# Each DMA transposition of u (128 x 1024) issued as two of 512 columns, in a fused retention and SoLU kernel on one core

## The chip, the cores and the metric

The kernel runs on 1 core of one Trainium2 chip. The metric is the device time of one execution in microseconds (us), measured outside the profiler; less is better. Before the change it is 212.93 us, the median of 3 runs (211.94 to 213.08). Where a profile is quoted, it is one execution taken by the hardware profiler, and its span runs from the first to the last instruction.

## The reference

A retention step (attention without softmax, with a decaying causal mask) feeds a feed-forward layer with the SoLU activation and a normalisation:

```python
# q, k, v: (8, 8, 576, 64) float32
scores = (1 / sqrt(64)) * (q @ k.T)
gamma  = 1 - 2 ** (-5 - head)
ret    = scores * where(i >= j, gamma ** (i - j), 0)
x      = (ret @ v) as (4608, 512)          # 8 batches x 576 tokens, 8 heads x 64

h  = x @ w_in                              # (4608, 1024)
e  = exp(h - max(h));  sm = e / sum(e)
s  = h * sm
ln = (s - mean(s)) / sqrt(var(s) + 1e-6) * g_ln
out = ln @ w_out                           # (4608, 512) float32
```

The inputs are drawn at random, x 0.1 for q, k and v.

## The kernel before, in words

The 4608 tokens are cut into 36 chunks of 128 tokens: for each pair of batches eight full chunks and one that holds the last 64 tokens of both. A chunk passes through some thirty small steps, each a Python function of the chunk's number:

- `ld` (L265 to L275) loads q, k and v of a chunk, 256 KB each, by three DMAs on SyncE's queue (L270 and L274).
- `cq`, `ck`, `cv` convert them to 16 bits with the decay factored in, on GpSimd, VectorE or ScalarE.
- `tq`, `tr` and `eq`, `er` transpose q and k on TensorE and copy the result out. For some later chunks `kd` (L322) transposes k by a DMA instead, 128 x 512 to 128 x 4 x 128 (L326), and `kq` (L330) does the same for q of one chunk (L331).
- `sc`, `mk`, `av`, `fs`, `ex` compute scores, mask, ret @ v and the carried state; `m1` computes h = x @ w_in on TensorE; `mx`, `xp`, `so` compute max, exp and u = -h * e (`so`, VectorE, L527).
- u (128 tokens x 1024, 16 bits, 256 KB) has to be transposed before the last product. For 19 of the 36 chunks `tu` (TensorE) and `eu` (a copy out of PSUM) do this, and for the last chunk steps of its own in halves. For the other 16, `du` (L592) does it by one DMA on SyncE's queue (L594).
- `m2` multiplies uT by w_out in 8 blocks of 128 rows, two matmuls a block through the helper `product` (L256). `st` scales the result by 1/sqrt(var) on ScalarE (L615) and stores it on SyncE's queue (L621, L623).

The order of all steps on all engines is a list written out by hand (ORDER, L24): a token such as `du:23` issues that step for chunk 23, and every engine works through its own instructions in the order of this list. SyncE issues all loads, all stores and all DMA transpositions, in that order too: an instruction of SyncE that waits holds all those behind it. Buffers are named by hand as well (RINGS and SLOTS): u and uT have 5 buffers each, the loads 6 or 7, the output 4. Each DMA signals its landing on one of eight semaphores, taken in turn, and waits before its issue for the DMA that used the same semaphore eight DMAs earlier.

The 16 uses of `du` begin at 95.4 us. They are thin at first (chunks 12, 14, 16, 18) and dense in the second half of the list.

Of the kernel before, what the change touches and what calls it, by code (L numbers as in the profile page):

```python
# [146 lines left out]
def kernel(  # L147
# [10 lines left out]
    nc = tc.nc  # L158
# [71 lines left out]
    def ring(pool, shape, dtype, name):  # L230

        at = int(next(slots[name]))
        assert at < RINGS[name]
        return pool.tile(shape, dtype, tag=f"{name}_{at}", name=name, bufs=1)
# [5 lines left out]
    T = {}  # L240
# [350 lines left out]

    def du(n):  # L592
        uT = ring(utp, [P, NF, P], F16, "uT")
        nc.sync.dma_start_transpose(out=uT, in_=T.pop(("u", n)))  # L594
        T["uT", n] = uT

    def eu(n, e="a"):
# [268 lines left out]
```

## Time and profile before

| what | value |
|---|---|
| time, median of 3 runs | 212.93 us (211.94 to 213.08) |
| profiled execution, its span | 210.9 us |
| TensorE (PE) busy | 194.3 us, 92% |
| VectorE (DVE) busy | 181.4 us, 86% |
| ScalarE (ACT) busy | 170.5 us, 81% |
| GpSimd (POOL) busy | 157.2 us, 75% |
| granted TensorE clock | 1.000 |
| SyncE's DMA queue, packets' time | 99.7% of 16 engines' span |
| DMA transpositions of u (L594) | 16, issued from 95.4 to 198.2 us |
| DMA transpositions of k (L326) and q (L331) | 7 and 1 |

The profiled execution's own time outside the span is not recorded; the span lies 2.0 us under the median of the runs.

How to read the profile: PE is TensorE's matmuls, PEld its weight loads, SPq is SyncE's queue, which issues DMAs. A line number is that of the source before the change. In the groups, `out<-in xcount | busy, mean ns | idle before` gives the work of one line and the time in which its engine stood idle in front of it. In the timeline of SyncE a row has its start, its length and the DMA that it issues; the length covers the issue and whatever held it up. In the chain of waits each row has its start, its length and the work to which that time is put down. A wait reads as who waited, for whom, the total in us, how often, and the longest.

### The profile page before, as it was taken

The numbers are of one execution on the slowest core, as the hardware profiler recorded it, in microseconds if no ns is written. First come the engines' busy times: TensorE is split into PE (matmuls) and PEld (weight loads), VectorE is DVE, ScalarE is ACT, GpSimd is POOL, SyncE is SP. The second block draws the span as 40 slices with busy tenths as digits, with TensorE's granted clock in tenths as the row PEclk, the third lists the DMA queues.
The fourth block names the chain that finished last, engine by engine and source line by source line (L and its number), as shares of the span: only waits on it lengthen the run. The fifth ranks groups of instructions, "written<-read, shape, count | busy, mean of one in ns | idle before, by whom it ended". The sixth has DMA issues, their size and how long they took to land.

```text
span 210.9 us, 7583 instructions
## 1 busy us (share of the span) xinstructions
PE 194.3 (92%) x3125; PEld 124.0 (59%) x3125; DVE 181.4 (86%) x323; ACT 170.5 (81%) x299; POOL 157.2 (75%) x226
## 2 busy tenths in 40 slices
PE   0887798999999999999999999999999998999992
PEld 0464476575666657657566667575656654565562
DVE  0486999979997999899989999999879998999760
ACT  2424999898979999999898978999679976677981
POOL 5377899676689899888839798879999977545620
PEclk9999999999999999999999999999999999999999
DMA  5999998999898989999999899999989999899754
GB/s 134 257 330 294 258 272 290 253 209 299 224 215 258 265 215 273 221 251 230 208 275 197 205 231 238 273 226 206 179 143 256 210 166 205 156 247 199 154 174 149
DMA packets 110834, 47.71 MB, mean 226 GB/s; under 512 B 94536, under 2 KB 104784, under 8 KB 110800
## 3 DMA queue, kind: packets, MB, share of 16 engines
q1 hardware_dynamic: 110480, 47.07, 99.7%
q8 instruction: 24, 0.39, 0.8%
q10 hardware_dynamic: 320, 0.16, 0.3%
q14 instruction: 10, 0.08, 0.2%
HBM read 32.54 MB, written 9.44 MB: 199 GB/s over the span
## 4 chain that ended last, share of the span: by engine, by line
PE 55%; SPq 14%; DMA 8%; DVE 8%; POOL 7%; ACT 3%; issue 3%; DVEq 0%; POOLq 0%
PE o L256 21%; PE h L256 18%; SPq L274 5%; SPq L270 5%; DMA w_out<-in_moe_w_out_dram 3%; PE tp L251 3%; PE sc L381 3%; PE lp L251 3%; DMA qkT<-k 2%; PE x L456 2%; POOL v L279 2%; SPq L789 2%; DMA qf<-in_q_dram 2%; PE x L256 2%; SPq L779 2%
## 5 line engine op out<-in xcount | busy, mean ns | idle before, releaser
L256 PE MATMUL h<-w_in,xT 128*64 128x512 f16 x560 | 66.9, 380 | 0.1
L256 PE MATMUL o<-w_c,uT 128*64 128x512 f16 x480 | 56.9, 380 | 0.0
L394 DVE TENSOR_TENSOR ret<-sc,tris 128x512 f16<-128x512 f32 x72 | 46.1, 682 | 2.8 <-PE sc L381 2.5
L256 PEld LDWEIGHTS <-xT 128*64 128x64 f16 x576 | 31.5, 110 | 23.1 <-issue 0.7
L512 DVE TENSOR_REDUCE nm<-h 128x1 f32<-128x1024 f32 x35 | 42.6, 1216 | 2.8 <-PE h L256 2.7
L256 PEld LDWEIGHTS <-uT 128*64 128x64 f16 x560 | 31.0, 110 | 23.0 <-issue 0.6
L527 DVE SCALAR_TENSOR_TENSOR u<-h,e 128x1024 f16<-128x1024 f32 x35 | 42.5, 1215 | 1.5 <-ACT e L518 1.4
L518 ACT ACTIVATE e<-h,nm 128x1024 f32<-128x1024 f32 x35 | 39.4, 1125 | 5.0 <-DVE nm L512 3.1
L432 POOL TENSOR_TENSOR s<-t,small 128x512 f16<-128x512 f32 x32 | 33.9, 1063 | 7.4 <-DVE t L420 6.1
L555 ACT ACTIVATE sq<-u,su 128x1024 bf16<-128x1024 f16 x30 | 34.8, 1159 | 2.0 <-DVE u L527 2.0
L581 POOL TENSOR_TENSOR rs<-w,mhalf 128x1 f32<-128x1 f32 x36 | 20.3, 570 | 20.7 <-DVE w L572 17.2
L290 POOL TENSOR_TENSOR q<-qf,small 128x512 f16<-128x512 f32 x30 | 31.2, 1043 | 5.4 <-DMA qf<-in_q_dram 5.1
L279 POOL TENSOR_TENSOR v<-vf,small 128x512 f16<-128x512 f32 x30 | 31.7, 1062 | 2.8 <-DMA vf<-in_v_dram 2.5
L615 ACT ACTIVATE o_sb<-o,rs 128x512 f32<-128x512 f32 x35 | 24.0, 692 | 4.5 <-POOL rs L581 3.2
L243 ACT COPY qkT<-tp 128x512 f16<-128x512 f16 x42 | 23.0, 599 | 5.0 <-PE tp L251 4.9
L243 ACT CAST xT<-x 128x512 f16<-128x512 f32 x29 | 17.1, 593 | 3.1 <-PE x L256 2.8
L251 PE MATMUL tp<-ident,q 128*64 128x128 f16 x232 | 12.4, 230 | 6.0 <-POOL q L290 5.5
L243 ACT CAST k<-kf 128x512 f16<-128x512 f32 x17 | 10.5, 626 | 7.7 <-DMA kf<-in_k_dram 7.7
L456 PE MATMUL x<-ret,v 128*64 128x128 f16 x288 | 14.8, 222 | 2.1 <-DVE ret L394 1.5
L251 PEld LDWEIGHTS <-q 128*64 128x64 f16 x280 | 11.0, 115 | 8.9 <-POOL q L290 5.7
L381 PE MATMUL sc<-qkT 64*128 64x128 f16 x288 | 14.7, 223 | 1.3 <-DMA qkT<-k 0.8
L444 POOL TENSOR_TENSOR s<-t,small 128x256 f32<-128x256 f32 x24 | 15.3, 638 | 0.9 <-DVE t L420 0.8
(87 smaller groups left out, 272.1 us busy)
## 6 DMA issues: line engine op xcount, KB each, us to landing
qf<-in_q_dram SPq DMA_DIRECT2D x36, 256.0 KB, 5.1
kf<-in_k_dram SPq DMA_DIRECT2D x36, 256.0 KB, 5.0
vf<-in_v_dram SPq DMA_DIRECT2D x36, 256.0 KB, 5.5
out_dram<-o_sb SPq DMA_DIRECT2D x35, 256.0 KB, 4.2
w_in<-in_moe_w_in_dram SPq DMA_DIRECT2D x4, 512.0 KB, 6.0
w_out<-in_moe_w_out_dram SPq DMA_DIRECT2D x4, 512.0 KB, 6.5
uT<-u SPq DMA_TRANSPOSE x16, 4.6
out_dram<-o_sbh SPq DMA_DIRECT2D x2, 64.0 KB, 1.8
```

Source lines behind the costliest of these rows:

```text
L243: (engine.copy if engine is nc.scalar else engine.tensor_copy)(out=out, in_=in_)
L251: nc.tensor.transpose(out=out[w], in_=in_[:, w], identity=ident)
L256: nc.tensor.matmul(out=out[w], lhsT=lhsT[:, w], rhs=rhs, start=start, stop=stop, skip_group_check=True,)
L279: engine.tensor_tensor(out=dst, in0=T.pop((key, n)), in1=table.unsqueeze(2).to_broadcast([P, H, D]), op=ALU.mult,)
L290: ENG[e].tensor_tensor(out=dst.rearrange("p (a h) d -> p h a d", h=2), in0=T.pop(("qf", n)).rearrange("p (h a) d -> p h a d", h=2), in1=ta ...
L394: nc.vector.tensor_tensor(out=r, in0=s, in1=m, op=ALU.mult)
L432: nc.gpsimd.tensor_tensor(out=s16, in0=t.unsqueeze(2).to_broadcast([P, 4, 2, D]), in1=gd.unsqueeze(3).to_broadcast([P, 4, 2, D]), op=ALU.mult,
L512: nc.vector.tensor_reduce(out=nm, in_=T["h", n], axis=AX.X, op=ALU.max, negate=True)
L518: nc.scalar.activation(out=e, in_=T["h", n], func=ACT.Exp, bias=T.pop(("nm", n)), accum_out=s)
L527: nc.vector.scalar_tensor_tensor(out=u, in0=T.pop(("h", n)), scalar=-1.0, in1=T.pop(("e", n)), op0=ALU.mult, op1=ALU.mult, accum_out=su,)
L555: nc.scalar.activation(out=s, in_=T.pop(("v", n)), func=ACT.Square, scale=-float(DFF), bias=T.pop(("su", n)), accum_out=ss,)
L615: nc.scalar.activation(out=o_sb, in_=T.pop(("o", n)), func=ACT.Copy, scale=T.pop(("rs", n)))
```

## The change

`du` takes its tile of u, allocates the same buffer for uT, and issues two DMAs in place of one: columns 0 to 511 go into blocks 0 to 3 of uT, columns 512 to 1023 into blocks 4 to 7. Both stand on SyncE's queue, one directly behind the other. The tokens in ORDER, the buffers and all other steps are unchanged.

```diff
     def du(n):
         uT = ring(utp, [P, NF, P], F16, "uT")
-        nc.sync.dma_start_transpose(out=uT, in_=T.pop(("u", n)))
+        u = T.pop(("u", n))
+        for i in range(2):
+            nc.sync.dma_start_transpose(
+                out=uT[:, 4 * i : 4 * i + 4], in_=u[:, 512 * i : 512 * i + 512]
+            )
         T["uT", n] = uT
```

In the program that results, SyncE has 16 instructions more. The first half carries the waits of the old DMA (for u, and for the last product that read the buffer of uT). The second half waits only for the DMA eight places earlier in the queue. On TensorE the product `m2` waits for the first half before its first block and for the second half before its fifth. The order of the instructions on every engine is otherwise as it was; the DMAs behind each split take the next semaphores of the eight in turn.

## The prediction

> **What bounds the kernel now.** I read the page first, then the busy time by stage, then the chain of waits, and last the timeline of SyncE, the only queue that the edit touches. From the page:
>
> ```profile
> span 210.9 us, 7583 instructions
> ...
> PE 55%; SPq 14%; DMA 8%; DVE 8%; POOL 7%; ACT 3%; issue 3%; DVEq 0%; POOLq 0%
> ...
> L256 PE MATMUL o<-w_c,uT 128*64 128x512 f16 x480 | 56.9, 380 | 0.0
> ```
>
> TensorE carries most of the chain, SyncE's queue comes second. The third line is the consumer of the transposed u: 480 matmuls, and TensorE stood idle 0.0 us in front of them, so no uT arrives late today. By stage (us; then PE, PEld, DVE, ACT, POOL busy with counts; clock; DMA share and GB/s):
>
> ```profile
> 139.00:177.00 38.00, 37.24 (x617) 23.71 (x613) 35.41 (x61) 31.51 (x57) 32.85 (x48) 1.00 1.08 201
> 177.00:195.00 18.00, 17.18 (x224) 9.48 (x222) 16.69 (x29) 13.57 (x24) 10.12 (x14) 1.00 1.09 199
> 195.00:211.00 16.00, 12.08 (x158) 7.51 (x154) 7.76 (x23) 10.47 (x21) 4.74 (x12) 1.00 0.58 159
> ```
>
> From 139 to 195 us TensorE is idle for 0.76 + 0.82 us only, at full clock. Whatever stops TensorE there is paid at the end, nearly one for one. The DMA share of 1.08 says that packets were under way on all 16 engines together nearly all the time. What stops TensorE, from the waits:
>
> ```profile
> PE sc L381 <- DMA qkT<-k: 0.8, 1, 0.8
> ...
> POOL q L279 <- DMA qf<-in_q_dram: 2.6, 1, 2.6
> ```
>
> and from the chain (start, us, what):
>
> ```profile
> 173.57 5.15 DMA qkT<-k
> 178.71 0.05 issue
> 178.76 0.40 PE sc L381 x8
> ...
> 199.71 3.45 PE o L256 x32
> 203.16 0.45 PE lph L251 x16
> 203.61 1.73 PE o L256 x16
> 205.33 1.77 PE oh L256 x32
> ```
>
> So there is one place where SyncE already sets the end: the transposition of k issued at 173.57, landed at 178.71, on which the score matmuls wait. It stands behind everything that SyncE issued earlier, five transpositions of u in this stage among them. After 178.76 the chain is TensorE alone.
>
> **The price of one split.** The two kinds of transposition that the trace has, by source line (min/median/max ns):
>
> ```profile
> L594 SPq DMA_TRANSPOSE uT<-u x16: 1238/1440/3667, 95.4 to 198.2; - x16
> ...
> DMA to landing us min/median/max: 3.4/4.6/5.7
> ...
> L326 SPq DMA_TRANSPOSE qkT<-k x7: 1195/1224/2036, 143.0 to 176.9; - x7
> ```
>
> L326 moves 512 columns, the very shape of a half; L594 moves 1024. SyncE needs at least 1195 ns for the one and 1238 for the other: its time hardly depends on the columns. So a half is priced at 1.20 us, the first half replaces the old instruction, and the second adds 1.20 and about 0.08 to the next row (152.47 + 1.30 to 153.89 below is 0.12, 169.15 + 1.39 to 170.60 is 0.06): 1.28 us each, 16 x 1.28 = 20.5 us of SyncE. Bytes do not change. On the DMA engines I take two halves to cost what one whole costs: the program's own 512-column transpositions show nothing else.
>
> **How much of it is hidden.** SyncE works in order, and many of its rows last longer than their floor (1.24 for a whole transposition, 1.20 for 512 columns, 0.53 for a store, 0.57 for a load at L274). I call the excess a hold: the DMA queue is full and SyncE waits for room. That is an inference, from the DMA share above; the waits view names compute engines for some of these rows, without a pattern. A hold can hide the extra issue in front of it, since SyncE would stand there anyway. The decisive stage:
>
> ```profile
> 140.74 2.16 SPq L594 DMA_TRANSPOSE uT<-u  x1
> ...
> 146.94 3.53 SPq L594 DMA_TRANSPOSE uT<-u  x1
> ...
> 152.47 1.30 SPq L594 DMA_TRANSPOSE uT<-u  x1
> 153.89 2.04 SPq L326 DMA_TRANSPOSE qkT<-k  x1
> ...
> 158.17 1.14 SPq L621 DMA_DIRECT2D out_dram<-o_sb  x1
> 159.42 1.33 SPq L326 DMA_TRANSPOSE qkT<-k  x1
> ...
> 162.81 3.67 SPq L594 DMA_TRANSPOSE uT<-u  x1
> ...
> 169.15 1.39 SPq L594 DMA_TRANSPOSE uT<-u  x1
> 170.60 0.57 SPq L274 DMA_DIRECT2D qf<-in_q_dram  x1
> 171.22 1.30 SPq L274 DMA_DIRECT2D kf<-in_k_dram  x1
> 172.56 0.90 SPq L274 DMA_DIRECT2D vf<-in_v_dram  x1
> 173.57 1.72 SPq L326 DMA_TRANSPOSE qkT<-k  x1
> ```
>
> Five splits: 5 x 1.28 = 6.40 us. Holds on other rows: 0.84 (153.89), 0.61 (158.17), 0.13 (159.42), 0.73 (171.22), 0.33 (172.56), 0.52 (173.57), together 3.16. Holds on the split rows themselves: 0.92, 2.29 and 2.43 at 140.74, 146.94 and 162.81, almost nothing on the other two. Two bounds follow for the delay at 173.57:
>
> - All holds hide. Carried forward: 1.28 - 0.92 = 0.36, gone at 146.94; 1.28 - 0.06 = 1.22 after 152.47, 0.38 after 153.89, gone at 158.17; nothing left of 162.81; 1.13 after 169.15, 0.40 after 171.22, 0.07 after 172.56, gone at 173.57. The delay is 0.
> - Holds on split rows hide nothing, because the second half waits for the same room as the whole did and spends its 1.20 after that: 6.40 - 3.16 = 3.24.
>
> I take the middle. A half asks for half the room, so the first half can go in during the hold, but the second still ends after it: half of 1.28 hidden at each of three long holds, 1.92. The delay is 6.40 - 1.92 - 3.16 = 1.32, rounded to **1.3 us**, at the transposition on which TensorE waits with nothing to spare (landed 178.71, used 178.76). The load of 170.60 feeds GpSimd, which stood 2.6 us for it; it is late by about as much and ends on the same chain.
>
> **Before 139 us** the four splits are followed by larger holds:
>
> ```profile
> 99.78 2.89 SPq L621 DMA_DIRECT2D out_dram<-o_sb  x1
> 102.77 1.33 SPq L594 DMA_TRANSPOSE uT<-u  x1
> ...
> 109.70 3.26 SPq L621 DMA_DIRECT2D out_dram<-o_sb  x1
> ```
>
> A store of 0.53 that lasts 2.89 or 3.26 us has over 2.3 us of hold; one split in front of each needs 1.28. Price 0; if that cover is gone, 1.28 falls on the loads behind each, whose buffers are several chunks ahead.
>
> **After 177 us** six more splits and the last one:
>
> ```profile
> 180.84 1.05 SPq L270 DMA_DIRECT2D qf<-in_q_dram  x1
> ...
> 183.32 2.68 SPq L594 DMA_TRANSPOSE uT<-u  x1
> 186.10 1.00 SPq L621 DMA_DIRECT2D out_dram<-o_sb  x2
> 187.20 3.93 SPq L594 DMA_TRANSPOSE uT<-u  x2
> 191.22 0.53 SPq L621 DMA_DIRECT2D out_dram<-o_sb  x1
> 191.86 2.69 SPq L594 DMA_TRANSPOSE uT<-u  x2
> ...
> 198.19 1.24 SPq L594 DMA_TRANSPOSE uT<-u  x1
> ```
>
> From 179.5 to 194.55 there are 6 x 1.28 = 7.7 us more and holds of about 1.44 (183.32) + 1.45 (the pair at 187.20, 3.93 less two floors) + 0.4 (180.84) = 3.3, so the last of this group is issued 4.4 us later. It would end at about 199; the quickest landing after an issue's start is 3.4 us, so it lands near 194.55 - 1.3 + 3.4 + 4.4 = 201.0 instead of 196.6. Its product is the second half of the chain's row 199.71 + 3.45, begun at 201.4, and its second four blocks are wanted only 0.87 later; the 1.3 us of before moves that use back too. Hidden, by 0.4 to 2 us. The transposition of 198.19 would land at 201.6; queue and split make it late by 1.6 at most, against 203.61 for its product. Hidden as well. Taken at 0, up to 1.0 if the queue is slower than this.
>
> **TensorE** gets 16 more waits, one at the fifth block of each product. The row of 3.45 us holds two products whose uT came by DMA: 1.73 each, the same as 203.61's, so a wait already met costs nothing that can be seen. Beginning on the first half early gains nothing where the idle time was 0.0.
>
> **Sum.** Span 210.9 + 1.3 + 0 + 0 = 212.2. The median of the runs is 212.93, 2.0 us above the profiled span; I keep these 2.0: **214.2 us**.
>
> **The rivals.**
>
> 1. Everything is hidden. The holds are the queue's, not SyncE's; SyncE issues more in time that it spends waiting. For it: the DMA share of 1.08 and the sum of holds in the decisive stage, 9.0 us against 6.4. Against it: behind the split of 169.15 comes the load of 170.60, which has no hold and would be 1.13 late even with every hold counted, and GpSimd stands for it. Time: 212.9 to 213.4.
> 2. Nothing is hidden at the split rows: 3.24, and the tail's 1.0 may follow: 216.2 to 217.2. For it: 1.20 us of issue comes after the room is there. Against it: the queue was filled by DMAs that would themselves be issued later.
> 3. Faster. SyncE's time goes by columns after all, 0.62 for a half. Then the split costs nothing, the first half enters the queue while the hold for the second runs, and the row of 173.57 moves forward. It decides as soon as two halves together cost less than a whole with its hold; the price is the idle time of TensorE in the two stages, 0.8 to 1.6 us: 211.3 to 212.1. Against it: 1195 next to 1238.
>
> The Trainium skill, "DMA: Bandwidth & Descriptors", section "Why a DMA increments its semaphore by 16 and not by 1", would speak for the third: its table of sequencer times gives, for the generations before the newest, one push command for every tile of a transposition (262,144 cycles for 8,192 tiles). By that rule a half would need half the time and the sum would be 0 or below; the trace does not agree, with 1195 against 1238 ns.
>
> That the split does not take place, or that the second half waits for the first to land, I count as nothing: both halves are separate instructions with separate completion counts.
>
> **How the numbers follow.** The forecast's case (part hidden, 0.7 to 2.3 us) has 0.43, the first rival 0.28, the second 0.19, the third 0.10. The range leaves out the third's better part and the top of the second: 212.2 to 216.8; the likeliest case alone spans 213.6 to 215.2. Half a per cent is 1.06 us, about what can be told from no change here. Slower takes five sixths of the forecast's case and all of the second: 0.36 + 0.19 = 0.55. Faster takes the third: 0.10. The rest, 0.35, is the same.
>
> **What would show it.** SyncE has 32 transpositions of u at a floor near 1.2 us each; at 0.6 the third rival is right. The transposition of k that stood at 173.57 starts 1 to 2 us later, and the wait of the score matmuls grows from 0.8 to about 2. If its start has not moved, the first rival holds; at 3 us or more, the second. The holds at 146.94 and 162.81 shrink. No idle time stands before the products of uT; if it does, the tail was mis-sized. The forecast is wrong if TensorE's idle time grows in stages where I price nothing, before 139 or after 195.

## The result and the profile after

| | time, median | lowest to highest |
|---|---|---|
| before | 212.91 us (4 runs) | 211.94 to 213.08 |
| after | 221.83 us (4 runs) | 220.35 to 222.91 |

The ratio is 1.0427, with a 95% interval from 1.037 to 1.0485: 8.9 us slower, and 5 us above the top of the predicted range. The profiled execution of after took 222.91 us, its span is 221.2.

The lines of the page of after that answer to those of before, with the row of the transposition from the part on DMA issues:

```profile
span 221.2 us, 7600 instructions
...
PE 41%; SPq 15%; DMA 15%; DVE 12%; POOL 8%; ACT 4%; issue 3%; DVEq 0%; POOLq 0%; ACTq 0%
...
L256 PE MATMUL o<-w_c,uT 128*64 128x512 f16 x480 | 57.8, 381 | 2.6 <-DMA uT<-u 2.6
...
uT<-u SPq DMA_TRANSPOSE x32, 3.1
```

TensorE's share of the chain fell from 55 to 41%, and the waits for a DMA to land grew from 8 to 15%. The products of uT, which stood 0.0 us for a DMA, now stand 2.6. A half takes 3.1 us (median) from its issue to its landing, where a whole took 4.6, so the second half, issued 1.3 us behind the first, lands at about the time at which the whole did.

The stages of after (us; then PE, PEld, DVE, ACT, POOL busy with counts; clock; DMA share and GB/s):

```profile
139.00:177.00 38.00, 35.41 (x590) 22.13 (x584) 33.88 (x57) 30.18 (x56) 32.10 (x47) 1.00 0.96 184
177.00:195.00 18.00, 14.63 (x216) 8.59 (x216) 13.85 (x24) 11.34 (x20) 8.62 (x11) 1.00 0.89 165
```

TensorE was idle for 0.76 and 0.82 us in these stages and is now idle for 2.59 and 3.37, at full clock. The DMA engines carry less at a time (share 0.96 and 0.89, from 1.08 and 1.09). Had the DMA engines become the limit, a higher share would be expected; the lower one points to what feeds them.

What the engines of after wait for:

```profile
POOL q L290 <- DMA qf<-in_q_dram: 8.9, 5, 2.5
...
PEld L256 <- DMA uT<-u: 5.7, 9, 1.2
...
POOL q L279 <- DMA qf<-in_q_dram: 4.8, 1, 4.8
...
PE sc L381 <- DMA qkT<-k: 3.0, 1, 3.0
...
PE o L256 <- DMA uT<-u: 2.6, 4, 1.0
```

Loads (`qf`), the transposition of k and those of u are late together. What they have in common is SyncE's queue and the DMA engines, and the engines carry less than before.

The timeline of SyncE in after (start, length, DMA; x2 is both halves in one row):

```profile
95.38 3.81 SPq L596 DMA_TRANSPOSE uT<-u  x2
...
101.25 2.63 SPq L625 DMA_DIRECT2D out_dram<-o_sb  x1
...
111.21 1.99 SPq L274 DMA_DIRECT2D vf<-in_v_dram  x1
113.30 1.63 SPq L625 DMA_DIRECT2D out_dram<-o_sb  x1
...
144.71 2.55 SPq L596 DMA_TRANSPOSE uT<-u  x2
...
148.67 1.50 SPq L625 DMA_DIRECT2D out_dram<-o_sb  x1
...
152.29 3.24 SPq L596 DMA_TRANSPOSE uT<-u  x2
...
157.29 1.26 SPq L625 DMA_DIRECT2D out_dram<-o_sb  x1
158.61 2.53 SPq L596 DMA_TRANSPOSE uT<-u  x2
161.25 1.20 SPq L326 DMA_TRANSPOSE qkT<-k  x1
...
164.52 1.25 SPq L625 DMA_DIRECT2D out_dram<-o_sb  x1
165.88 1.29 SPq L326 DMA_TRANSPOSE qkT<-k  x1
...
169.96 3.83 SPq L596 DMA_TRANSPOSE uT<-u  x2
...
174.52 1.72 SPq L326 DMA_TRANSPOSE qkT<-k  x1
...
176.95 2.54 SPq L596 DMA_TRANSPOSE uT<-u  x2
179.54 0.57 SPq L274 DMA_DIRECT2D qf<-in_q_dram  x1
180.16 0.62 SPq L274 DMA_DIRECT2D kf<-in_k_dram  x1
180.83 0.67 SPq L274 DMA_DIRECT2D vf<-in_v_dram  x1
181.60 1.96 SPq L326 DMA_TRANSPOSE qkT<-k  x1
...
210.61 2.55 SPq L596 DMA_TRANSPOSE uT<-u  x2
```

And rows of before that the prediction did not show:

```profile
95.44 2.27 SPq L594 DMA_TRANSPOSE uT<-u  x1
...
108.70 0.90 SPq L274 DMA_DIRECT2D vf<-in_v_dram  x1
...
144.29 0.53 SPq L621 DMA_DIRECT2D out_dram<-o_sb  x1
...
151.88 0.53 SPq L621 DMA_DIRECT2D out_dram<-o_sb  x1
```

Put beside each other, row for row, SyncE falls further behind from stage to stage, though not at every row (it is 3.6 us late at 113.30 and 2.0 at 115.04). The first transposition of u starts at 95.44 before and 95.38 after. The fifth starts at 140.74 and 144.71 (4.0 late), the transposition of k for which TensorE waits at 173.57 and 181.60 (8.0 late), the last one of u at 198.19 and 210.61 (12.4 late). From the first to the last, 15 splits at 1.28 us are 19.2 us; 12.5 of them came through.

The chain of waits of after shows where the rest of the program pays:

```profile
115.04 4.82 DMA uT<-u
...
163.26 3.81 DMA kf<-in_k_dram
...
180.16 4.29 DMA kf<-in_k_dram
...
186.39 3.96 DMA qkT<-q
...
192.57 5.54 DMA uT<-u
...
211.90 2.54 DMA uT<-u
214.49 1.05 PE o L256 x8
```

Before, the chain had two DMAs between 40 and 211 us, the transposition of k at 173.57 and this one:

```profile
136.34 4.56 DMA qf<-in_q_dram
```

Now there are six, and three of them have nothing to do with u. The last row is the second half of the last uT: it lands at 214.44, and the last four blocks of that product start at once behind it. TensorE stands in front of them.

### The profile page after: what moved, and what is told of

Read it like the earlier page. It is cut to its first block, busy times and chain, and to the rows that moved or that the text cites. A ratio compares the mean times of both kernels' runs of the same rounds, so it can differ in the third digit from the quotient of the medians.

```text
span 221.2 us, 7600 instructions
## 1 busy us (share of the span) xinstructions
PE 197.4 (89%) x3125; PEld 124.4 (56%) x3125; DVE 182.9 (83%) x323; ACT 170.9 (77%) x299; POOL 158.0 (71%) x226
## 4 chain that ended last, share of the span: by engine, by line
PE 41%; SPq 15%; DMA 15%; DVE 12%; POOL 8%; ACT 4%; issue 3%; DVEq 0%; POOLq 0%; ACTq 0%
PE o L256 17%; PE h L256 11%; DMA uT<-u 6%; SPq L274 6%; SPq L270 4%; DMA w_out<-in_moe_w_out_dram 4%; DMA kf<-in_k_dram 4%; DVE ret L394 3%; PE tp L251 3%; PE sc L381 2%; PE lp L251 2%; DVE nm L512 2%; DVE u L527 2%; SPq L793 2%; DMA qkT<-q 2%
## 5 line engine op out<-in xcount | busy, mean ns | idle before, releaser
L256 PE MATMUL h<-w_in,xT 128*64 128x512 f16 x560 | 67.9, 386 | 0.0
L256 PE MATMUL o<-w_c,uT 128*64 128x512 f16 x480 | 57.8, 381 | 2.6 <-DMA uT<-u 2.6
L256 PEld LDWEIGHTS <-uT 128*64 128x64 f16 x560 | 30.4, 110 | 27.0 <-DMA uT<-u 5.7
L256 PEld LDWEIGHTS <-xT 128*64 128x64 f16 x576 | 32.2, 112 | 23.4 <-issue 1.2
L432 POOL TENSOR_TENSOR s<-t,small 128x512 f16<-128x512 f32 x32 | 34.6, 1084 | 7.9 <-DVE t L420 6.9
L251 PE MATMUL tp<-ident,q 128*64 128x128 f16 x232 | 12.4, 230 | 6.2 <-POOL q L290 5.6
L381 PEld LDWEIGHTS <-qkT 64*128 64x128 f16 x288 | 8.5, 96 | 13.6 <-issue 4.7
L456 PEld LDWEIGHTS <-v 128*64 128x64 f16 x288 | 11.8, 113 | 7.3 <-issue 3.1
```

The lines of the kernel that those rows point to most:

```text
L251: nc.tensor.transpose(out=out[w], in_=in_[:, w], identity=ident)
L256: nc.tensor.matmul(out=out[w], lhsT=lhsT[:, w], rhs=rhs, start=start, stop=stop, skip_group_check=True,)
L381: nc.tensor.matmul(out=s[e][:, hp], lhsT=qkT[dd, 1, hp], rhs=qkT[dd, 0, hp], start=True, stop=True,)
L432: nc.gpsimd.tensor_tensor(out=s16, in0=t.unsqueeze(2).to_broadcast([P, 4, 2, D]), in1=gd.unsqueeze(3).to_broadcast([P, 4, 2, D]), op=ALU.mult,
```

## The experiments

Three explanations were to be told apart: SyncE's time for 16 more instructions; the halves themselves, on the DMA engines or at the product that waits for two landings; and a queue without room. Each time below is a median, with the ratio to before and its 95% interval.

**A second instruction that moves almost nothing.** u is transposed whole, as before; behind it SyncE transposes 128 columns of it again, into a buffer that nobody reads.

```diff
-        nc.sync.dma_start_transpose(out=uT, in_=T.pop(("u", n)))
+        u = T.pop(("u", n))
+        nc.sync.dma_start_transpose(out=uT, in_=u)
+        spare = utp.tile([P, 1, P], F16, tag="spare", name="spare", bufs=5)
+        nc.sync.dma_start_transpose(out=spare, in_=u[:, 0:P])
```

> Each u is transposed whole, by one DMA as before, and behind it SyncE issues one more transposition of 128 x 128 into a spare tile that nobody reads. Theory A (SyncE's time for an instruction of this kind, about 1.25 us whatever it moves, is the cost, since the queue is in order and has no time to spare): as slow as the change, +7 to +10 us over before, 220 to 223. Theory B (the DMA engines: two halves cost them more, or land later, than one whole): an eighth of the data more, +0 to +2 us. Theory C (TensorE's extra wait for the second half): +0 to +1 us, since uT arrives by one DMA again.

223.46 us, 1.0543 (1.0485 to 1.0601). The view of the spare tile (min/median/max ns, first and last start):

```profile
L597 SPq DMA_TRANSPOSE spare<-u x16: 1217/1227/2064, 95.3 to 212.8; - x16
```

An eighth of u's columns takes SyncE as long as a half or a whole, and the program pays at least as much as for the change. No product waits for this DMA and u isn't cut, so the price is paid here without any halves.

**The same with a plain copy.** In place of the second transposition, a copy of the same 128 x 128 elements.

```diff
+        spare = utp.tile([P, P], F16, tag="spare", name="spare", bufs=5)
+        nc.sync.dma_start(out=spare, in_=u[:, 0:P])
```

> As the run with the spare transposition, but the extra DMA is a plain copy of the same 128 x 128 piece. A plain DMA takes SyncE 0.53 to 0.62 us where a transposition takes 1.25. Theory A: about half of the cost, +3 to +5 us. If what costs is a transposition as such (its place in the DMA queue, or on the DMA engines): +0 to +1 us.

216.81 us, 1.0239 (1.0177 to 1.03). The spare tile again:

```profile
L597 SPq DMA_DIRECT2D spare<-u x16: 581/587/1538, 99.1 to 206.1; - x16
```

0.59 us of SyncE in place of 1.23, and 5.0 us of time in place of 11.6: the time follows what the instruction costs SyncE.

**The splits by stage.** Only the first four uses of `du`, only the next five, only the last seven are split; the edit of the first is shown, the others differ in the condition (`20 <= n < 28`, `n >= 28`).

```diff
+        parts = 2 if n < 20 else 1
+        w = NF // parts
+        for i in range(parts):
+            nc.sync.dma_start_transpose(
+                out=uT[:, w * i : w * i + w], in_=u[:, P * w * i : P * w * (i + 1)]
+            )
```

> Only the four transpositions before 139 us (chunks 12, 14, 16, 18) are split. The prediction priced these at 0. In the traces the load that started at 136.34 us starts 2.7 us later with the change. If that delay stays to the end: +2 to +3 us, 215 to 216. If the holds behind 139 us take it up again: +0 to +0.7 us.

> Only the five transpositions from 139 to 177 us (chunks 20, 22, 23, 25, 27) are split. The prediction priced these at 1.3 us, its upper bound was 3.2. The traces show the transposition of k of 173.57 us moved by 8.0 us, of which 2.7 were there before the stage: +5 us if holds hide almost nothing (217 to 219); +1 to +2 if the delay of the earlier stage was what used up the holds.

> Only the seven transpositions after 177 us (chunks 28 to 34) are split. The prediction priced these at 0, at most 1.0. The run with the first four cost 3.1 us, that with the middle five 6.4. If every split costs its share of SyncE's time and nothing takes it up, the three add up to the change (about +9.5): +1 to +4 us here. If the tail hides them as predicted: 0 to +0.5.

| split | time | ratio | above before | for each split |
|---|---|---|---|---|
| first 4, from 95 us | 214.94 | 1.014 (1.0076 to 1.0204) | 3.0 us | 0.74 us |
| next 5, 140 to 170 us | 218.2 | 1.0287 (1.0221 to 1.0354) | 6.1 us | 1.22 us |
| last 7, from 179 us | 214.93 | 1.0109 (1.0065 to 1.0152) | 2.3 us | 0.33 us |

(Above before is the ratio less one, times 212.) The three sum to 11.4 us against 8.9 for the change, just within what the intervals together allow. All three stages pay, and the middle one pays nearly the whole of each split, 1.22 of 1.28 us.

**Relieving SyncE through ScalarE.** The stores of the chunks from 12 on are issued by ScalarE, in the kernel after and in the kernel before.

```diff
-            nc.sync.dma_start(out=dst[0, c * P : (c + 1) * P, :], in_=o_sb)
+            (nc.scalar if n >= 12 else nc.sync).dma_start(out=dst[0, c * P : (c + 1) * P, :], in_=o_sb)
```

> The change, and the stores of the output of chunks 12 to 34 are issued by ScalarE instead of SyncE (same bytes, same DMA engines; about 0.55 us of ScalarE each). SyncE gets 23 x 0.6 = 14 us back. Theory A (SyncE's issue time sets the end): most of the change's loss comes back, 213 to 217. Theory B (DMA engines): no change, 220 to 222, or worse for ScalarE's time.

> The kernel before, with the same stores on ScalarE. Theory A: SyncE was already the limit behind 139 us, so -1 to -4 us, 208 to 211, unless ScalarE (busy 45 of 56 us there) becomes the limit. Theory B: 0 or slower.

222.74 us, 1.0438 (1.0334 to 1.0541), and 215.81 us, 1.0149 (1.008 to 1.0219). Both were expected to gain and neither did. The view of the output tile in the second, and the chain of the first (an execution of 224.34 us, the longest of its four):

```profile
L621 ACTq DMA_DIRECT2D out_dram<-o_sb x21: 338/339/428, 105.2 to 209.7; - x21
```

```profile
131.06 8.32 DMA vf<-in_v_dram
139.46 0.35 ACTq L625
...
164.14 3.51 DMA qf<-in_q_dram
167.73 0.34 ACTq L625
```

Each store costs ScalarE 0.34 us of its own, and in the first kernel it waits there for loads that SyncE issued (131.06, 164.14): the eight landing semaphores are taken in turn by both queues, so a store of ScalarE waits for the last DMA that used its semaphore, whoever issued it. The second kernel shows hardly any such wait. The pair moves a cost to ScalarE; it can't tell the theories apart, and says only that this is no way out.

**Half of the data.** One DMA of 512 columns in place of 1024, so that the number of instructions is that of before; the second half of u isn't transposed, and the product reads the first half twice.

```diff
+        nc.sync.dma_start_transpose(out=uT[:, 0:4], in_=u[:, 0:512])
...
+            b = c % 4 if T.get(("half", n)) else c
+            product(o, uT[:, b], w[:, c], c == 0, c == NF - 1)
```

> Each u gets one DMA as before, but it transposes the first 512 columns alone; the second half of the last product reads the first half's blocks once more, so the output is not the reference's. SyncE's time stays (1.20 instead of 1.24 us), the DMA engines' work for u is halved. Theory A: within 1 us of before, 211 to 213. Theory B (the DMA engines are the limit): -2 us or more, 209 or less.

211.26 us, 0.9965 (0.9919 to 1.0012): with half the bytes of every transposition of u gone, nothing that can be measured is gained. That says less than it seems: TensorE was idle for only 1.6 us between 139 and 195 us before, so little more than that could be won there. The DMA engines' work on u costs the kernel before no more than this. SyncE's rows do get shorter, as the section on the holds shows; the time so freed goes into waits, mostly until u or an output tile is ready (gaps above 0.25 us between its rows: 17.7 us in all, from 3.6).

**Quarters.** Four DMAs of 256 columns for each u.

```diff
+        for i in range(4):
+            nc.sync.dma_start_transpose(
+                out=uT[:, 2 * i : 2 * i + 2], in_=u[:, 256 * i : 256 * i + 256]
+            )
```

> Each transposition of u as four DMAs of 256 columns, 48 SyncE instructions more than before the change. Theory A (SyncE's issue time, about 1.25 us an instruction whatever the columns, and half of it or more paid): 60 us of issue, the first 20 of which cost 9; the other 40 cost between the same half and the whole: 241 to 262 us, and rows of L594 near 1.22 us each. Rival D (a hold is room that the queue lacks, so that small pieces fit in and most of the extra issue is hidden; the change paid only what did not fit): a second halving costs no more than the first, 221 to 231 us.

260.55 us, 1.2318 (1.2247 to 1.239). The tile uT in this kernel:

```profile
L596 SPq DMA_TRANSPOSE uT<-u x64: 1177/1243/2225, 93.4 to 247.8; - x64
```

Theory A holds, and D's time is far off. 48 more instructions of 1.24 us are 60 us of SyncE, and 48 us of time are paid for them, 80%. The first 20 us cost 9, the next 40 cost 39: once the little slack is gone, SyncE's time is nearly the program's time. SPq has 24% of the chain, from 14%. Part of the 48 us may be TensorE's own: its granted clock was 0.83 from 200 to 250 us in this execution, and it was busy for 211.1 us, from 194.3.

**Fewer DMAs on SyncE, with nothing moved elsewhere.** The stores of two neighbouring chunks (the same rows of two batches) become one DMA behind the second; 15 instructions of SyncE go, the orders of the other engines stay. In the kernel after, and in the kernel before:

```diff
+            T[pr] = moe.tile([P, 2, DM], FP, tag="o_pr", name="o_pr", bufs=3)
+        o_sb = T[pr][:, j]
...
+                both = out.rearrange("(b s) m -> b s m", b=B)[bs[0] - j : bs[0] - j + 2]
+                nc.sync.dma_start(
+                    out=both[:, c * P : (c + 1) * P, :].rearrange("b t m -> t b m"),
+                    in_=T.pop(pr),
+                )
```

> The change, and the stores of two neighbouring chunks (the same rows of two batches) written as one DMA behind the second of them: 15 stores of SyncE fewer, about 10 of them after 90 us; the other engines keep their instructions and orders. Theory A (SyncE's time, about half of it paid): 10 x 0.6 to 1.0 us with their holds = 6 to 10 us less of SyncE, 3 to 5 us less in all: 217 to 219 us. Rival E (the cost lies in the halves themselves, at the consumers or on the DMA engines, and not in what else SyncE issues): 221 to 222.5 us.

> The kernel before the change with the same paired stores. Theory A: SyncE is late already, so that its time is worth something here too, but TensorE is idle for only 2 to 3 us between 95 and 195 us: 210.5 to 212.5 us, no more than 2.5 below before. Rival E: 212 to 213 us.

219.44 us, 1.0337 (1.0282 to 1.0393), and 212.48 us, 1.0002 (0.9962 to 1.0042). The split kernel wins back 2.4 us by the medians and 1.9 by the ratios, whose intervals just overlap, when ten stores that have nothing to do with u leave its queue. That is half a microsecond less than Theory A had, and below the 221 that E had. In the kernel before the same relief is worth nothing: SyncE's time is not the limit there, and the next 20 us make it one. No kernel here is measurably faster than before.

**What the holds are.** One candidate was tried: the trace has 24 instruction fetches of 16 KB, each one packet on one DMA engine, and the large holds near 96, 101, 110 and 117 us each overlap one. So SyncE was given a 16 KB packet of its own behind each transposition.

```diff
         nc.sync.dma_start_transpose(out=uT, in_=T.pop(("u", n)))
+        nc.sync.dma_start(
+            out=w_out32.rearrange("p c m -> p (c m)")[0:1],
+            in_=q[0, 0, 0:64, :].rearrange("s d -> (s d)").unsqueeze(0),
+        )
```

> The kernel before the change; behind each transposition of u SyncE also copies 16 KB in one row (64 rows of q, to one partition of a buffer that is no longer needed). Same places and number as the copies of 128 x 128 (216.8 us, 0.58 us of SyncE each), but all bytes on one DMA engine, as in the 16 KB instruction fetches. Theory H (a hold is SyncE waiting for the one DMA engine that a 16 KB packet occupies, so that it is no spare time): each copy brings a hold of 1 us or more behind it, 16 us or more of holds beyond the 30 of before, and 219 us or more. Rival F (holds come from the sum of what is queued, and one packet of 16 KB adds nothing to that): holds stay at about 30 us, and the time at 215 to 217.5 us.

216.57 us, 1.0246 (1.0165 to 1.0327), inside F's bounds. The tile's view:

```profile
L595 SPq DMA_DIRECT2D w_out<-in_q_dram x16: 223/381/1099, 96.6 to 204.7; - x16
```

The holds did not grow (next table): Theory H falls in this form, for a packet on SyncE's own queue. The copies are paid as any instruction is: 16 x 0.38 = 6.1 us of SyncE, 4.7 us of time.

The sum of the holds, worked out for each kernel from its timeline of SyncE between its first and its last transposition of u, as each row's length less the floor of its kind, where that is above 0 (1.24 for u, 1.20 for k and q, 0.53 for a store, 0.56 to 0.61 for a load, a spare instruction's median), 84 rows before and 99 after:

| kernel | SyncE time added, us | holds, us |
|---|---|---|
| before | 0 | 30.1 |
| 16 copies of one packet | 6.1 | 29.3 |
| 16 plain copies | 9.4 | 28.8 |
| 16 spare transpositions | 19.6 | 27.4 |
| after (halves) | 20 | 25.6 |
| quarters | 60 | 23.2 |
| half of the columns, one DMA for each u | 0 | 18.2 |

The last row is the only one with less data in the queue, and it has the smallest sum. The rows of u that lasted 3.53 and 3.67 us before (146.94 and 162.81) are these in that kernel:

```profile
146.86 1.74 SPq L595 DMA_TRANSPOSE uT<-u  x1
...
161.45 1.93 SPq L595 DMA_TRANSPOSE uT<-u  x1
```

So the holds depend on the data that are queued, and hardly on the number of instructions. They also have a place: 14 of the 84 rows of before stand directly behind a chunk's load of v, and these carry 19.5 of the 30.1 us (15.3 of 25.6 after). They are no waits for data or for a semaphore: on all 21 rows of before with a hold above 0.5 us, what the DMA reads, the buffer that it writes and its semaphore were free before the row began. The instruction fetches are not cleared: 12 of the 13 in this stretch overlap one of these 21 rows, where fetches shifted along the same timeline would hit 8 on average, and no run changes them. How much of a hold is due to which stays open.

## Why the prediction was wrong, step by step

- **The price of one split: right.** 1.28 us was forecast. Where no hold lies on the row, one transposition took 1.30 (152.47) and two halves take 2.53 (158.61). With 128, 256, 512 and 1024 columns SyncE needed at least 1217, 1177, 1195 and 1238 ns. The third rival falls with it. The rule that the prediction set beside it, a push for every tile of a transposition (the Trainium skill, "DMA: Bandwidth & Descriptors", section "Why a DMA increments its semaphore by 16 and not by 1"), is not seen in these rows: eight times the columns cost 2% more (1217 to 1238 ns), not eight times as much.
- **No cost on the DMA engines, no cost of 16 more waits on TensorE: right.** Half the columns gain nothing that can be measured, and a spare transposition that nobody waits for costs as much as the split.
- **"A hold can hide the extra issue in front of it": the step that failed.** In place the holds behaved as forecast, and better: the five split rows of the decisive stage grew by 2.6 us together (12.05 to 14.69), where 6.40 - 1.92 = 4.48 were forecast. But the other rows of the stage, which were to give back 3.16, cost 1.4 more instead: the stage took 32.83 us from 140.74 to 173.57 and takes 36.89 from 144.71 to 181.60, 4.06 more. The holds that were named did shrink (2.04 to 1.20 at the transposition behind the third split, 1.30 to 0.62 at the load of k); more came back on rows that had none: the stores at 148.67 (1.50, from 0.53) and 157.29 (1.26, from 0.53), the transposition at 174.52 (1.72, from 1.22). A hold that an instruction covers in one place turns up in another, and their sum hardly falls: 30.1 to 25.6 us with 20 us added, 23.2 with 60. Holds were counted as spare time of SyncE; they made room for 4.5 of 20 us, and for 6.9 of 60.
- **Before 139 us, priced at 0: wrong for the same reason.** The two stores that were to hide a split each fell from 2.89 to 2.63 and from 3.26 to 1.63, but the load ahead of the second grew from 0.90 to 1.99. Four splits of 5.1 us made SyncE 4.0 late at 140.74. They cost 3.0 us when they are the only ones, and TensorE's idle time from 95 to 139 us grew from 0.5 to 1.4 us, the prediction's own sign that it was wrong.
- **The decisive wait: the right place, the wrong size.** The transposition of k was to start 1.3 us late, at 3 or more by the second rival; it started 8.0 late, 4.0 from each stage. The score matmuls' wait grew from 0.8 to 3.0, where 2 was forecast; the rest of the delay had by then become other waits (the loads of 163.26 and 180.16 in the chain), which the sum had no term for.
- **After 177 us, priced at 0, at most 1.0: wrong.** The working put the last landing at 201.6 with 203.61 for its use; SyncE was 12.4 us late there, and it lands at 214.44 with TensorE waiting. The last seven splits alone cost 2.3 us.
- **The sum.** Stage by stage, 0 + 1.3 + 0 were forecast, and 3.0 + 6.1 + 2.3 measured where each is split alone. The second rival, nothing hidden at the split rows, was nearest in number, by luck: the split rows did hide 3.8 of their 6.40 us, and it too let the other holds hide 3.16 and took the stage before as free. The 2.0 us between span and median were kept rightly: 1.7 in the profiled execution of after.

Shown by the runs: the cost is SyncE's issue time, whatever the instruction moves, and the holds make little room for it; their sum falls when the data of u are halved. The prediction's "queue is full" agrees with that, but not its step from there to spare time. Only argued: why a hold that is covered in one place comes back in another.

## What to carry to other kernels

On a queue that issues back to back, price each further DMA at its full issue time, and look for slack only where its consumers stand with data to spare; a row that was longer than its floor was little slack here. A DMA transposition cost SyncE the same for 128 as for 1024 columns, so make few and large ones. A spare instruction that nobody waits for, put where the change would add one, prices such a change in one run.

## What was not expected of the hardware

- SyncE's time for a DMA transposition does not depend on its size between 128 and 1024 columns of 128 partitions: medians of 1227 ns for the spare 128 columns, 1243 for the quarters and 1258 for the halves, and 1238 at least for a whole, against 587 for a plain copy of 128 x 128 and 381 for 16 KB in one row.
- Holds hardly shrink when instructions are added: 23 to 30 us in the same stretch of the program with 0 to 60 us added, but 18.2 with half of u's data. The Trainium skill, "Perfetto Trace Analysis", section "DMA Instruction — HWDGE (DVE, Sync)", says that such a row covers the wait for a shared descriptor generator and the generation, and starts only when the semaphores are met. The rows of before agree with the start: on all 21 with a hold above 0.5 us the data were ready before the row began. Whether the hold lies in that wait or in the generation no run here shows.
- Landing semaphores tie two queues together: a store on ScalarE's queue was issued only when a load of SyncE had landed, 8.32 us after that load's own issue (139.46 in its chain).
